# Values in two transfers, scales by one product with the identity, and a planner with other costs

## The chip, the cores and the metric

The kernel runs on one core of a Trainium2 chip. Its time is the device time of one execution in microseconds; the number compared is the median over runs. A profile of one further execution shows what each engine did: PE (TensorE, matmuls), PEld (its weight loads), ACT (ScalarE), DVE (VectorE), POOL (GpSimd) and SP (SyncE, which issues the DMAs here).

## The reference

Chunked attention with memory tokens, then a mixture of eight experts in which every token goes through every expert, weighted by a routing matrix that is normalised eight times by rows and columns.

```python
q, k, v: (4, 8, 768, 64)      mem_k, mem_v: (4, 8, 8, 64)
for c in range(24):                     # chunks of 32 rows
    k_ctx = k[:, :, max(0, 32*c - 16) : min(768, 32*c + 40)]   # v alike
    k_full = concat([mem_k, k_ctx])     # v alike
    a = softmax(q_c @ k_full.T / 8)
    out[:, :, chunk c] = a @ v_full
x = out.transpose(0, 2, 1, 3).reshape(3072, 512)

P = exp(x @ w_gate - max)               # (3072, 8)
for _ in range(8):
    P /= P.sum(1, keepdims=True) + 1e-9
    P /= P.sum(0, keepdims=True) + 1e-9
    P *= 3072 / 8
for e in range(8):                      # w1 (8, 512, 1024), w2 (8, 1024, 512)
    y += P[:, e:e+1] * (maximum(x @ w1[e], 0) @ w2[e])
```

## The kernel before

**Two kinds of work.** The attention goes over 24 blocks of 128 queries (six for each of the four batches, all eight heads together). A block has loads of q, k, a few extra rows of k (`load_extra`) and v; transposes of q and k on TensorE (tiles tq, tk, tx); small products of 32 rows for each chunk, head and block (`scores`, tile sp); maximum, difference and exponential; a transpose back (ta); the small products with the values (`values`, tile xp); division by the sum, and a transpose on VectorE into the tile xg, which holds 256 tokens. The experts go over 48 pairs of an expert and a unit of 512 tokens. All these products are made of numbers split into two float16 parts, high and low, so each product is three passes over matmuls of 256 columns (line 1676), and products of two by two blocks are made with seven block products in place of eight, with sums taken beforehand. The first unit (`first_unit`, tile pp for the hidden layer at line 2117) and the outputs of expert 0 (`plain_output`, tile yp at line 2200, 512 columns) are made without these sums, since the sums are not ready yet.

**Splitting.** `split` (line 540) makes the two parts of an operand: ScalarE writes the scaled high part (line 545), then VectorE the rest (line 553). `plain1` and `plain2` call it for expert 0's weights, in four parts fp = 0 to 3 of 512 KB each. `cut` (line 643) makes the sums of weights on GpSimd (line 651).

**Scales.** Every operand is scaled by a power of two that comes from the largest element, or from a bound on it. `scales` (line 462) turns a column of one bound per partition into one scale on all 128 partitions. In the kernel before: VectorE reduces to one column (473); TensorE transposes the column to a row (525, tile row); VectorE reduces the row (534) and rounds to a power of two (478, 479); TensorE spreads the number over 128 partitions by a product with ones (511, tile sp_x or sp_w); VectorE makes the inverse (484, 485). For the values, blocks 0 and 1 use a sum of absolute values on ScalarE (`total_v`, 1032), blocks 2 and 3 a maximum on VectorE (`most`, 1022).

**The values' tile.** It holds two windows in its 128 partitions: rows 0 to 63 for one chunk and rows 64 to 127 for the chunk two further on, each with eight memory rows ahead and 56 rows of v. `go_v` (line 987) loads them by four DMAs of 56 rows (8 heads x 256 bytes each). The memory rows are loaded once for a batch and slot by two small DMAs (`go_m`) and copied by GpSimd (`copy_m` 975, `take_m` 985); a later block of the same batch in the same slot finds them there.

**What sets the order.** The whole program is laid out beforehand by a planner (`Plan`, line 98). Every piece of work is a task with an engine, a cost in microseconds, those that it waits for, a priority (a due time) and its buffers. `Plan.run` walks a simulated clock, and for each engine takes the task that could start first, or the one with the lowest due time among those that can start now; each engine then has its instructions in that fixed order. The planner also models the DMA pipe (`dma=` cost of a transfer, `LANDS`, `READY`, `BEHIND`), the port that VectorE and GpSimd share (`port`, `held`), and the fetching of TensorE's own instructions (`count` and `earliest`: after 161 instructions and every 256 after that a fetch is asked for, which lands `FETCH` us later). Where it sees TensorE idle for over 0.4 us it puts in warming matmuls (`pad`, line 137; `fill`, line 452, tile warm), until the attention is over (`turn` sets `plan.fill` to None). The due times come from `START`, `TURN`, `UNIT`, `NEED` and the like (line 374).

Of the kernel before, what the change touches and what calls it, by code (L numbers as in the profile page):

```python
# [25 lines left out]
LANDS = 0.7  # L26
# [4 lines left out]
BLOCK = 256  # L31
ASKS = 161
HELD = 288
FETCH = 1.4
QUEUED = 6.0
FREE = 0.3


class Task:


    __slots__ = ("eng", "cost", "fn", "prio", "left", "ready", "end", "then", "takes", "frees", "n", "dma", "start", "size", "port")
# [55 lines left out]
class Plan:  # L98
# [16 lines left out]
    def add(self, eng, cost, fn, deps=(), prio=0.0, bufs=(), takes=None, frees=None, dma=0.0,  # L115
            size=0, port=None, since=0.0):
# [3 lines left out]
        t.size = size  # L120
# [16 lines left out]
    def pad(self, now, at):  # L137

        for banks in self.free.values():
            if banks and banks[0][0] <= now + 0.2:  # L140
                n = int((at - now - 0.1) * 0.8 / 0.11)
                if n > 0:
                    _, bank = heappop(banks)
                    self.fill(bank, n)
                    heappush(banks, (now + 0.11 * n + 0.2, bank))
                    self.count(2 * n, now, 0.11 * n)
# [12 lines left out]
    def earliest(self, t, at):  # L159


        for end, landed in self.fetches:
            if t.size and self.counted + t.size > end:
                at = max(at, landed - t.cost * (end - self.counted) / t.size)
        return at

    def run(self):
# [4 lines left out]
        for t in self.tasks:  # L172
            if t.left == 0:
                heappush(waiting[t.eng], (t.ready, t.n, t))
        left = len(self.tasks)
        while left:
            best = None
            for e in self.ENGINES:
# [26 lines left out]
                if pick is not None and (best is None or pick[0] < best[0]):  # L205
                    best = pick
            assert best is not None, "no task can start"
            at, t, heap = best
            if t.eng == "PE" and self.fill is not None and at - clock["PE"] > 0.4:
                self.pad(clock["PE"], at)  # L210
            heap[:] = [x for x in heap if x[2] is not t]
            heap.sort()
# [23 lines left out]
            else:  # L236
                clock[t.eng] = t.end = at + t.cost
            t.fn()
# [6 lines left out]
            lag = 0.0 if t.dma else 0.2 if t.eng == "PE" else 0.12  # L245
            for s in t.then:
                s.left -= 1
                late = lag
                if s.eng == t.eng and not t.dma:
                    late = 0.0  # L250
# [4 lines left out]
                if s.left == 0:  # L255
                    heappush(waiting[s.eng], (s.ready, s.n, s))
# [4 lines left out]
def tile_chunked_attn_sinkhorn_moe(  # L261
# [28 lines left out]
    P = 128  # L290
# [56 lines left out]
    idle = ident.bitcast(BF16)  # L347
    gate = amisc.tile([P, KT * E + CH - E], F32, name="gate")
# [25 lines left out]
    START, TURN, UNIT, AHEAD = 28.0, 62.0, 36.7, 48.0  # L374
# [77 lines left out]
    def fill(b, n):  # L452
        wp = banks(b).tile([P, 256], F32, tag=f"b{b}", name="warm")
        for _ in range(n):
            nc.tensor.matmul(wp, idle[:, 0:P], idle, start=True, stop=True)
# [6 lines left out]
    def scales(part, s, u, name, deps, prio, pool=None, shift=SHIFT):  # L462
# [26 lines left out]
        if pool is None:  # L489
# [14 lines left out]
        a = a[0:1]  # L504
        t = turned_max(m, a, t, pool, prio, name)
        t = add("DVE", 0.3, lambda: power(a), [t], soon, port=True)
        spread = bank(pool, [P, 1], f"sp_{name}")
        t = add(
            "PE",
            0.38,  # L510
            lambda: nc.tensor.matmul(spread.t, ones[0:1], a, start=True, stop=True),
            [t],
            prio - FIRM,
            takes=spread,
            size=4,
        )
        return add("DVE", 0.32, lambda: inverse(spread.t), [t], soon, frees=spread)

    def turned_max(m, a, t, pool, prio, name):
# [4 lines left out]
            0.35,  # L524
# [15 lines left out]
    def split(dst, src, s, deps, prio, costs, bufs=(), behind=()):  # L540
# [4 lines left out]
            lambda: nc.scalar.activation(dst(0), src(), AF.Copy, scale=s),  # L545
            deps,
            prio - 1.0,
            bufs,
        )
# [19 lines left out]
    def load(e, fp, which, prio, ahead="", since=0.0):  # L569
# [13 lines left out]
        cost = 1.7 if which == 1 else 1.5  # L583
# [18 lines left out]
    def total(fp, which, st, deps, prio):  # L602
# [11 lines left out]
        return add("ACT", 1.2, go, deps, prio, [st, first2[1]])  # L614
# [132 lines left out]
    def plain1(fp, st, ld, prio, behind=()):  # L747

        o = operands("w1", [P, 2, 7, 2, P], f"w1_0_{fp}")
        done = split(  # L750
# [5 lines left out]
            (1.15, 1.28),  # L756
            [st, o],
            behind,
        )
        wo[0, fp, 1] = (o, [done])  # L760
# [7 lines left out]
    def plain2(fp, st, ld, prio, before):  # L768

        done = split(  # L770
# [5 lines left out]
            (1.15, 1.28),  # L776
            [st, first2[fp]],
        )
        wo[0, fp, 2] = (first2[fp], [done])
# [15 lines left out]
    NEED = (4.0, 8.0, 29.0, 35.0)  # L795
# [32 lines left out]
    def load_extra(u):  # L828
# [10 lines left out]
        for n in range(n0, n0 + BU):  # L839
# [5 lines left out]
            def go(b=b, blk=blk, r0=r0, t0=t0):  # L845
# [7 lines left out]
                else:  # L853
# [10 lines left out]
                    dma=0.35,  # L864
# [7 lines left out]
        def part(r, loads, at, tx, takes):  # L872
            t = add("PE", 0.6, lambda: turn(r), loads, at, [kx, kxT], takes=takes, size=2 * HP)
# [1533 lines left out]
```

## Time and profile before

| | |
|---|---|
| median of three runs | 1905.94 us (1905.53 to 1907.52) |
| the profiled execution's own time | 1905.76 us |
| its span | 1904.0 us |
| granted TensorE clock, mean | 0.999 |
| busy ACT | 1028.3 us |
| DMA, mean over the span | 133 GB/s |

A profile page lists busy times; tables of stretches cut the span into windows; a list of waits says who waited for whom, with total, count and longest; a timeline lists instructions by start and length, merged where they repeat (xN); a bracket at its end tells how long the engine was idle before and what ended that. The chain is the work that ended last, followed back from the last instruction. "Issue" in it is time in which an engine waited for nothing that the profile shows. Durations of matmuls are modelled with their latency, so the rate of matmuls is read from their starts or their count in a stretch.

### The profile page before, as it was taken

Reading aid. Unit: us, or ns where it says so; the run is one execution under the profiler, and the core shown is the slowest. Engines: PE = TensorE matmul, PEld = TensorE weight load, DVE = VectorE, ACT = ScalarE, POOL = GpSimd, SP = SyncE. Lnnn points to the kernel's source line nnn. Section 1 sums busy time; section 2 is a strip of 40 time slices with the busy share of each in tenths; the row PEclk is TensorE's granted clock in tenths of the full one; section 3 lists DMA queues with packets and bytes.
Section 4 is the critical chain, followed back from the end, with each engine's and each line's share of the span. In section 5 each row is a group of like instructions: output and inputs, shape, how many; then the busy total and the mean of one; then the engine's idle time right before and its main releaser. Section 6 shows DMA issues by size and latency. Waiting matters only on the chain.

```text
span 1904.0 us, 46736 instructions
## 1 busy us (share of the span) xinstructions
PE 1889.6 (99%) x19471; PEld 1626.9 (85%) x19471; DVE 1455.4 (76%) x2417; ACT 1028.3 (54%) x2008; POOL 536.6 (28%) x576
## 2 busy tenths in 40 slices
PE   8999999999999999999999999999999999999999
PEld 6677676688888888888888888888888888888888
DVE  6886879778589866888679876897778885786575
ACT  6665455665466455556456545645555563554453
POOL 2430112544134211522224231342124231332112
PEclk9999999999999999999999999999999999999999
DMA  9967944543323541363235332255314633222322
GB/s 213 212 139 179 238 137 139 171 151 106 128 89 139 175 147 52 102 229 141 84 104 177 130 133 101 79 176 179 122 47 140 225 106 105 90 84 88 125 84 67
DMA packets 209101, 253.98 MB, mean 133 GB/s; under 512 B 108793, under 2 KB 142585, under 8 KB 204537
## 3 DMA queue, kind: packets, MB, share of 16 engines
q1 hardware_dynamic: 208888, 251.00, 42.3%
q8 instruction: 152, 2.49, 0.6%
q14 instruction: 61, 0.49, 0.1%
HBM read 187.51 MB, written 63.44 MB: 132 GB/s over the span
## 4 chain that ended last, share of the span: by engine, by line
PE 95%; DMA 2%; DVE 2%; issue 0%; ACT 0%; SPq 0%; POOL 0%; ACTq 0%; POOLq 0%; DVEq 0%
PE px L1676 25%; PE yx L1676 23%; PE pz L1676 13%; PE yz L1676 12%; PE py L1676 6%; PE yy L1676 6%; PE yp L2200 5%; PE pp L2117 1%; PE xp L1212 1%; PE sp L1134 1%; PE ta L1201 1%; DMA w1fm<-in_moe_w_dram 0%; PE tk L1075 0%; DMA w1f<-in_moe_w_dram 0%; PE tq L1071 0%; DVE x L553 0%
## 5 line engine op out<-in xcount | busy, mean ns | idle before, releaser
L1676 PEld LDWEIGHTS <-w 128*128 128x128 f16 x7896 | 771.3, 98 | 91.8 <-issue 1.0
L1676 PEld LDWEIGHTS <-h 128*128 128x128 f16 x7056 | 690.3, 98 | 80.0
L1676 PE MATMUL px<-x,w 128*128 128x256 f16 x4512 | 548.0, 273 | 0.1
L2003 POOL TENSOR_TENSOR acc<-acc,y 128x256 f32<-128x256 f32 x252 | 265.0, 1059 | 872.6 <-ACT y L1978 860.1
L1676 PE MATMUL yx<-w,h 128*128 128x256 f16 x4032 | 467.5, 273 | 0.0
L1725 ACT ACTIVATE q<-px 128x256 f32<-128x256 f32 x376 | 141.9, 380 | 288.1 <-PE px L1676 282.8
L1676 PE MATMUL pz<-x,w 128*128 128x256 f16 x2256 | 278.2, 273 | 0.1
L1676 PE MATMUL yz<-w,h 128*128 128x256 f16 x2016 | 233.8, 273 | 0.0
L1897 DVE TENSOR_TENSOR h<-ss,h 128x1024 f16<-128x1024 f32 x160 | 212.0, 1327 | 3.0 <-ACT h L1872 3.0
L1872 ACT CAST h<-ss 128x1024 f16<-128x1024 f32 x168 | 174.2, 1040 | 51.5 <-DVE ss L1835 51.5
L1847 ACT ACTIVATE h<-c 128x768 f16<-128x768 f32 x168 | 140.8, 838 | 108.5 <-DVE c L1735 108.3
L1880 DVE SCALAR_TENSOR_TENSOR h<-c,h 128x768 f16<-128x768 f32 x168 | 167.9, 1000 | 18.4 <-ACT h L1847 18.4
L1835 DVE SCALAR_TENSOR_TENSOR ss<-c,ss 128x256 f32<-128x256 f32 x336 | 171.5, 510 | 7.6
L1735 DVE SCALAR_TENSOR_TENSOR c<-px,q 128x256 f32<-128x256 f32 x188 | 77.8, 421 | 88.9 <-PE px L1676 84.7
L1676 PE MATMUL py<-x,w 128*128 128x256 f16 x1128 | 139.2, 273 | 0.0
L2200 PE MATMUL yp<-w,h 128*128 128x512 f16 x576 | 130.9, 379 | 0.0
L1835 DVE SCALAR_TENSOR_TENSOR ss<-c,h 128x512 f32<-128x512 f32 x168 | 126.1, 750 | 0.0
L1978 ACT ACTIVATE y<-yx,pscale 128x256 f32<-128x256 f32 x168 | 79.3, 472 | 83.7 <-PE yx L1676 78.7
L1676 PE MATMUL yy<-w,h 128*128 128x256 f16 x1008 | 116.9, 273 | 0.0
L1735 DVE SCALAR_TENSOR_TENSOR c<-py,q 128x256 f32<-128x256 f32 x188 | 77.7, 420 | 45.4 <-PE py L1676 42.5
L2200 PEld LDWEIGHTS <-h 128*128 128x128 f16 x576 | 55.5, 98 | 59.8
L545 ACT ACTIVATE w<-ws,sw 128x1024 f16<-128x1024 f32 (+1 forms) x64 | 69.5, 1090 | 67.1 <-POOL ws L651 66.4
(168 smaller groups left out, 1763.1 us busy)
## 6 DMA issues: line engine op xcount, KB each, us to landing
x<-xkeep SPq DMA_DIRECT2D x28, 1792.0 KB
akeep<-acc SPq DMA_DIRECT2D x168, 256.0 KB
acc<-akeep SPq DMA_DIRECT2D x168, 256.0 KB
w1f<-in_moe_w_dram SPq DMA_DIRECT2D x36, 512.0 KB
w2f<-in_moe_w_dram SPq DMA_DIRECT2D x32, 512.0 KB
w1fm<-in_moe_w_dram SPq DMA_DIRECT2D x28, 512.0 KB
w2fm<-in_moe_w_dram SPq DMA_DIRECT2D x28, 512.0 KB
xkeep<-x SPq DMA_DIRECT2D x6, 1792.0 KB
```

The lines of the kernel that those rows point to most:

```text
L545: lambda: nc.scalar.activation(dst(0), src(), AF.Copy, scale=s),
L1676: nc.tensor.matmul(dst.t, a, b, start=(not more and n == 0), stop=(n == end), skip_group_check=more,)
L1725: lambda: nc.scalar.activation(t.t, src.t, AF.Copy, scale=DOWN),
L1735: lambda: nc.vector.scalar_tensor_tensor(c.t[:, o], src.t, DOWN, q.t, op0=ALU.mult, op1=ALU.add),
L1835: lambda: nc.vector.scalar_tensor_tensor(dst(), src(), 0.0, other(), op0=ALU.max, op1=op),
L1847: lambda: nc.scalar.activation(h.t[:, 0, 0:3], c.t, AF.Relu),
L1872: lambda: nc.scalar.copy(h.t[:, 0, 3:7], ss.t),
L1880: lambda: nc.vector.scalar_tensor_tensor(h.t[:, 1, 0:3].rearrange("p a n -> p (a n)"), c.t.rearrange("p a n -> p (a n)"), 0.0, h.t[:, 0, 0 ...
L1897: lambda: spare.tensor_tensor(h.t[:, 1, 3:7], ss.t, h.t[:, 0, 3:7], op=ALU.subtract),
L1978: (lambda: nc.scalar.activation(t.t, src.t, AF.Copy, scale=f))
L2003: lambda: nc.gpsimd.tensor_tensor(acc.t[:, cols], acc.t[:, cols], q.t, op=ALU.add),
L2200: nc.tensor.matmul(py.t, hf.t[:, hl, where[fh], o : o + P], room(fp, WIDE * wl + DM * fh, WIDE * wl + DM * (fh + 1)), start=(fp == 0 and i ...
```

## The change

Six things at once, all in the making of the program:

1. `go_v` loads two DMAs per block, of up to 120 rows, which run on over rows 64 to 71; `go_m` loads the memory rows once; a new task `again_m` on GpSimd copies them over rows 64 to 71 behind the two DMAs, for every block. `values` and the bounds wait for it.
2. `scales` sends the column, broadcast to 128 columns, through one product with the identity, which gives the row on every partition; one task on VectorE makes the maximum, the power and the inverse there. The routing's own maximum keeps the old way.
3. Tasks can have a second engine (`also`): the high halves of expert 0's weights, two of the key copies and the first unit's relu may go to GpSimd where the planner finds it free sooner. For parts 2 and 3 of w1, `split_aside` puts all of it on GpSimd, but for the high half, which either of ScalarE and GpSimd may copy.
4. Blocks 2 and 3 of the values use `total_v` on ScalarE.
5. The warming matmuls have 512 columns in place of 256.
6. The planner's costs and due times: DMAs, products, the fetch of instructions, lags between engines; `START` 28 to 26, `TURN` 62 to 58, `AHEAD` 48 to 44; the gate's weights are due at 22 in place of 30; the routing is due 50 us behind the start of its unit in place of 30.

```diff
-LANDS = 0.7
+LANDS = 0.8
+GATE = 22.0
-FETCH = 1.4
+FETCH = 2.4
+REFILL = 1.4
+BACKLOG = 0.5
+OVERLAP = 0.07
+LAG = 0.04
+ROUTE = 50.0
+BESIDE = (2, 3), ()
...
-            queued = min(0.8 * max(self.pipe - when, 0.0), QUEUED)
+            queued = min(BACKLOG * max(self.pipe - when, 0.0), QUEUED)
...
-                at = max(at, landed - t.cost * (end - self.counted) / t.size)
+                done = t.cost * (end - self.counted) / t.size
+                if at + done < landed:
+                    at = landed + REFILL - done
...
                 clock[t.eng] = t.end = at + t.cost
+                if self.fill is not None and t.eng in ("ACT", "DVE"):
+                    clock[t.eng] -= OVERLAP
...
-        wp = banks(b).tile([P, 256], F32, tag=f"b{b}", name="warm")
+        wp = banks(b).tile([P, 2, 256], F32, tag=f"b{b}", name="warm")
...
-    START, TURN, UNIT, AHEAD = 28.0, 62.0, 36.7, 48.0
+    START, TURN, UNIT, AHEAD = 26.0, 58.0, 36.7, 44.0
...
+            lambda: nc.tensor.matmul(
+                row.t, m.broadcast_to([P, P]), ident, start=True, stop=True
+            ),
...
+        def here():
+            nc.vector.tensor_reduce(a, row.t, axis=AX.X, op=ALU.max)
+            power(a)
+            inverse(a)
+
+        return add("DVE", 0.85, here, [t], soon, port=True, frees=row)
...
+    def split_aside(dst, src, s, deps, prio, bufs=(), behind=()):
+
+        a = add(
+            "POOL",
+            1.1,
+            lambda: nc.gpsimd.tensor_scalar(src(), src(), s, None, op0=ALU.mult),
...
+        def high():
+            if b.eng == "POOL":
+                nc.gpsimd.tensor_copy(dst(0), src())
+            else:
+                nc.scalar.copy(dst(0), src())
+
+        b = add("ACT", 1.15, high, [a], prio - 1.0, bufs, also=("POOL", 1.1))
+        return add(
+            "POOL",
+            2.2,
+            lambda: nc.gpsimd.tensor_tensor(dst(1), src(), dst(0), op=ALU.subtract),
...
-    NEED = (4.0, 8.0, 29.0, 35.0)
+    NEED = (4.0, 8.0, 25.0, 31.0)
...
+        def again_m():
+            nc.gpsimd.tensor_copy(vt.t[KW : KW + NM, :, :, 0:D], vt.t[0:NM, :, :, 0:D])
...
-            for c in range(CB):
+            for c in range(CP):
                 r = NM + (LC if first and c == 0 else 0)
-                m = KW - r - (RC if last and c == CB - 1 else 0)
+                m = P - r - (RC if last and c == CP - 1 else 0)
...
-        lv = lm + [add("SP", CB, go_v, lv, at, [vt], dma=2.7)]
+        t = add("SP", CP, go_v, lv, at, [vt], dma=2.3)
+        lv = [*lm, add("POOL", 1.1, again_m, [*lm, t], at, [vt])]
...
-            vfound.append(add("DVE", 1.35, most_less, lv, at, [vt], since=START + 2.0))
+            vfound.append(add("ACT", 1.2, total_v, lv, at, [vt, first2[1]], since=START + 2.0))
...
-        hi = add(
-            "ACT",
-            0.63,
-            lambda: nc.scalar.activation(h.t[:, 0, where], c.t[:, 0:2], AF.Relu),
-            read,
-            now[0],
-            [h, c],
-        )
+        hi = add("ACT", 0.63, high, read, now[0], [h, c], also=("POOL", 0.75))
...
-        urgent = begin(LATE) + 30.0
+        urgent = begin(LATE) + ROUTE
...
         (),
-        30.0,
-        dma=0.3,
+        GATE,
+        dma=0.8,
```

More of the change, by code (lines that the diff above doesn't have):

```diff
@@ L31, with engines @@
 BLOCK = 256
+GATE = 22.0
 ASKS = 161
 HELD = 288
-FETCH = 1.4
+FETCH = 2.4
 QUEUED = 6.0
+REFILL = 1.4
+BACKLOG = 0.5
+OVERLAP = 0.07
+LAG = 0.04
 FREE = 0.3
+SUMS = 0.0
+ROUTE = 50.0
+BESIDE = (2, 3), ()
 class Task:
-    __slots__ = ("eng", "cost", "fn", "prio", "left", "ready", "end", "then", "takes", "frees", "n", "dma", "start", "size", "port")
+    __slots__ = ("eng", "cost", "fn", "prio", "left", "ready", "end", "then", "takes", "frees", "n", "dma", "start", "size", "port", "also")
+    def engines(self):
+        return (self.eng,) if self.also is None else (self.eng, self.also[0])
 class Past:
@@ L244, in run @@
                     heappush(self.free[b.group], (b.end, b.bank))
-            lag = 0.0 if t.dma else 0.2 if t.eng == "PE" else 0.12
+            near = LAG if self.fill is not None else 0.12
+            lag = 0.0 if t.dma else 0.2 if t.eng == "PE" else near
             for s in t.then:
@@ L347, in tile_chunked_attn_sinkhorn_moe @@
     idle = ident.bitcast(BF16)
+    twice = idle[:, None, :].broadcast_to([P, 2, 2 * P])
     gate = amisc.tile([P, KT * E + CH - E], F32, name="gate")
@@ L452, in fill @@
     def fill(b, n):
-        wp = banks(b).tile([P, 256], F32, tag=f"b{b}", name="warm")
+        wp = banks(b).tile([P, 2, 256], F32, tag=f"b{b}", name="warm")
         for _ in range(n):
-            nc.tensor.matmul(wp, idle[:, 0:P], idle, start=True, stop=True)
+            nc.tensor.matmul(wp, idle[:, 0:P], twice, start=True, stop=True)
     plan.fill = fill
@@ L503, in scales @@
             return add("DVE", 1.7, everywhere, [t], prio, port=True)
[L504 to L507, printed above, removed]
+        row = bank(pool, [P, P], f"row_{name}")
         t = add(
             "PE",
-            0.38,
-            lambda: nc.tensor.matmul(spread.t, ones[0:1], a, start=True, stop=True),
+            0.15,
+            lambda: nc.tensor.matmul(
+                row.t, m.broadcast_to([P, P]), ident, start=True, stop=True
+            ),
             [t],
             prio - FIRM,
-            takes=spread,
+            takes=row,
             size=4,
         )
-        return add("DVE", 0.32, lambda: inverse(spread.t), [t], soon, frees=spread)
+        def here():
[3 more added lines that the diff above has]
+        return add("DVE", 0.85, here, [t], soon, port=True, frees=row)
     def turned_max(m, a, t, pool, prio, name):
@@ L544, in split @@
             costs[0],
-            lambda: nc.scalar.activation(dst(0), src(), AF.Copy, scale=s),
+            high,
             deps,
@@ L612, in go @@
             )
-        return add("ACT", 1.2, go, deps, prio, [st, first2[1]])
+        return add("ACT", 1.2, go, deps, prio, [st, first2[1]], since=SUMS)
     def scale_w(e, which, deps, prio, pool=None, shift=SHIFT):
```

172 lines of the change are left out of this document (94 added, 78 removed).

## The prediction

> **What bounds the kernel now.** I read the page's first lines, then the stretches of the span, then TensorE's waits, then the chain of waits over the first 60 us.
>
> ```profile
> span 1904.0 us, 46736 instructions
> ...
> PE 1889.6 (99%) x19471; PEld 1626.9 (85%) x19471; DVE 1455.4 (76%) x2417; ACT 1028.3 (54%) x2008; POOL 536.6 (28%) x576
> ```
>
> ```profile
> 47.90:58.10 10.20, 8.26 (x205) 6.41 (x203) 9.37 (x18) 8.23 (x15) 0.72 (x1) 1.00 0.84 143
> ...
> 110.00:280.00 170.00, 169.34 (x3056) 123.91 (x3057) 128.12 (x240) 91.45 (x191) 19.29 (x25) 1.00 0.74 186
> ...
> 500.00:700.00 200.00, 200.00 (x1835) 179.24 (x1833) 160.21 (x255) 109.36 (x210) 64.42 (x69) 1.00 0.37 127
> ```
>
> The columns behind a window are its length, the busy time and count of PE, PEld, DVE, ACT and POOL, the granted clock, the DMA share and GB/s. From 110 us on TensorE is busy throughout: 169.34 of 170.00 us, later 200.00 of 200.00 with 1835 matmuls, 109 ns apiece. Those matmuls stay, so little can be won behind 110 us: the change acts on the first 110 us, and a microsecond in which TensorE does nothing useful there is a microsecond of the span, since no slack comes later. Part of the busy time is padding (the group of the warming matmuls), and TensorE's longest waits come beside it:
>
> ```profile
> L455 PE MATMUL warm<-ident 128*128 128x256 bf16 x119 | 16.9, 291 | 1.6 <-POOL ident masks.py:199 1.6
> ```
>
> ```profile
> PE pp L2117 <- ACT w L545: 2.1, 1, 2.1
> ...
> PE sp L1134 <- issue: 1.2, 1, 1.2
> PE xp L1212 <- issue: 1.0, 1, 1.0
> PE pp L2117 <- issue: 0.8, 2, 0.5
> ...
> PE lp L1472 <- DMA gate<-in_moe_w_gate_dram: 0.7, 1, 0.7
> ```
>
> So 16.9 us of warming matmuls and 5.8 us in these waits (2.1 + 1.2 + 1.0 + 0.8 + 0.7) are what the change can bite on, some 23 us; the attention of the first blocks must come ahead of the first expert matmul, so most of the padding stays. The chain (start, length, what) shows the way to that matmul:
>
> ```profile
> 16.37 4.98 DMA v_pair<-in_v_dram
> 21.64 0.96 issue
> ...
> 27.44 1.33 ACT x L545 x2
> 28.78 2.09 ACT w L545 x2
> 31.19 0.81 PE pp L2117 x6
> 32.68 5.35 PE pp L2117 x36
> ...
> 65.91 0.79 PE xp L1212 x53
> ```
>
> Block 1's values land at 21.35 us (16.37 + 4.98). TensorE's first expert matmul starts at 31.19, 9.84 us later.
>
> **A: the first expert matmul.** The change loads each block's values in two transfers of up to 120 rows in place of four of up to 56, and then GpSimd copies eight memory rows over rows 64 to 71 (again_m), which the attention's last product waits for. Rows for both, from the timelines of SyncE and GpSimd:
>
> ```profile
> 8.27 8.61 SPq L993 DMA_DIRECT2D v_pair<-in_v_dram x8
> ```
>
> ```profile
> 17.67 2.12 POOL L985 COPY x_room<-v_pair 8x1024 f32<-8x1024 f32 x2
> 50.26 0.72 POOL L1368 TENSOR_TENSOR xt<-xg 128x256 f32<-128x256 f32 x1 [30.47 <-DVE xg L1253]
> ```
>
> One copy of eight rows is 1.06 us (2.12 / 2); with a handover it puts about 1.2 us between landing and product. The eight issues took SyncE 8.61 us; four are fewer, but the rows per block grow from 224 to 240, 7% more packets, so I let the landing come 0.3 us earlier (bounds: 1.0 earlier, 0.5 later). The product can thus start near 22.2 us. The 0.96 us of "issue" in its middle should not return: padding matmuls are now twice as wide, so TensorE has fewer instructions by then.
>
> Behind it lie division, transpose and the scale of x, in the timeline of VectorE:
>
> ```profile
> 23.62 0.69 DVE L1233 TENSOR_TENSOR xq<-xp,rec 128x512 f32<-128x512 f32 x1
> ...
> 24.34 1.11 DVE L1253 STREAM_TRANSPOSE xg<-xq 128x512 f32<-128x512 f32 x1
> 25.36 0.24 DVE L534 TENSOR_REDUCE most_of<-row_x 1x1 f32<-1x128 f32 x1
> 25.63 0.14 DVE L478 TENSOR_SCALAR most_of<-most_of 1x1 f32<-1x1 f32 x1
> ...
> 25.88 1.26 DVE L553 SCALAR_TENSOR_TENSOR w<-w1f,sw,w 128x1024 f16<-128x1024 f32 x1
> ...
> 27.25 0.16 DVE L485 RECIPROCAL sx<-ux 128x1 f32<-128x1 f32 x1
> 28.20 1.42 DVE L553 SCALAR_TENSOR_TENSOR x<-xg,sx,x 128x512 f16<-128x512 f32 x2 [0.79 <-ACT x L545]
> ```
>
> From the reduction at 25.36 to the end of the reciprocal at 27.41 are 2.05 us, because the half-done scale goes back to TensorE (the spreading product) and VectorE does a weight of 1.26 us meanwhile. Now one product of the broadcast column with the identity gives the row of maxima on all 128 partitions, and reduction, two steps of the power and two of the inverse are one task: 0.24 + 2 x 0.14 + 2 x 0.16, about 0.85 us. So: product (0.79) 22.2 to 23.0, division to 24.1 (0.69 and two small steps), transpose to 25.2, scale to 26.1, ScalarE's first half (1.33 / 2) to 26.8, VectorE's (1.42 / 2) to 27.5, handover: first expert matmul at 27.7 against 31.19. Term A: -3.5 us, bounds -5.0 (the copy hidden as well) and -0.5 (only part of the detour saved). ScalarE's 2.09 us of weights ahead of that matmul no longer stand there: the plain weights of parts 2 and 3 go to GpSimd, idle for 30.47 us before 50.26.
>
> **B: the clock.** 36 expert matmuls took 5.35 us from 32.68; at 109 ns they take 3.9, so 1.4 us are lost. The stretches say why:
>
> ```profile
> 32.00:34.00 2.00, 2.00 (x13) 1.50 (x11) 2.00 (x3) 0.00 (x1) 0.00 (x0) 0.51 1.06 166
> 34.00:36.00 2.00, 2.00 (x13) 1.52 (x12) 1.80 (x3) 0.99 (x2) 0.00 (x0) 0.63 1.02 230
> ```
>
> The granted clock falls to 0.51 and 0.63 right after the wait of 2.1 us. If the plan sees that gap, it pads it, or the gap is gone: term B -1.4 us, bounds -1.4 and 0. The Trainium skill ("TensorE: Matmul & The Clock Gate", What's actually happening) has the clock halve only after an idle window of about 3.4 us; here 2.1 us of idling were followed by a halved clock, so the trace speaks for less. By that rule the dip would have no tie to this gap, B would be 0 and the gain 1.4 us smaller.
>
> **C: the first output product (58.07 us).** It waits for w2, whose scale takes the same detour:
>
> ```profile
> 49.88 0.27 PE L525 MATMUL row_w<-ident,most_of 128*1 128x128 f32 x1
> ...
> 58.07 2.75 PE L2200 MATMUL yp<-w,h 128*128 128x512 f16 x12
> ```
>
> ```profile
> 52.66 0.17 DVE L485 RECIPROCAL sw<-uw 128x1 f32<-128x1 f32 x1
> ```
>
> From 49.88 to 52.83 are 2.95 us; the new way takes the product's 0.27, a handover of some 0.2 and 0.85, about 1.3, so 1.6 less. Two maxima of values leave VectorE for ScalarE, whose high halves of w2, relu and small key copies may go to GpSimd; the gate's weights are asked for earlier. In 47.9 to 58.1 TensorE's busy time is 1.94 us short of 10.20, of which 0.7 is the gate, and some of the busy time is padding. Term C: -1.7 us, bounds -3.5 and 0.
>
> **D: TensorE's own instructions.** The page's DMA queues:
>
> ```profile
> q8 instruction: 152, 2.49, 0.6%
> ```
>
> 152 packets for 2 x 19471 matmuls and weight loads are one per 256 instructions. I take the waits called "issue" for late ones of these; 2.0 us (1.2 + 0.8) are not in A. The planner's new costs for that fetch (2.4 us in place of 1.4, and 1.4 more where it ran dry) let it place a score block elsewhere; but a shifted plan can run dry at new places. Term D: -0.5 us, bounds -2.0 and +1.5.
>
> **E: what is added.** again_m runs for all 24 blocks, where blocks that kept their memory rows had nothing: 24 x 1.06 = 25 us of GpSimd, which is 28% busy. Queued behind it on GpSimd are the weights' sums (L651); on TensorE, whose order is fixed, everything after that block's product stands behind it. From block 6 on values land long before use, so it costs nothing there unless GpSimd lags; in the ramp it can. Term E beyond what A holds: +1.0 us, bounds 0 and +4.
>
> Routing later and the other planned costs behind 280 us lie beside a full TensorE: 0. If that cover failed, the first scaled accumulators would wait.
>
> Sum: -3.5 - 1.4 - 1.7 - 0.5 + 1.0 = -6.1 us. The profiled execution took 1905.76 us (span 1904.0 and 1.76 around it), 0.18 under the median of 1905.94: 1905.76 - 6.1 = 1899.66, and with the 0.18 that the median lies above it 1899.8 us.
>
> **Rivals.**
>
> *The gain is given back.* In the first 60 us the DMA engines are nearly full:
>
> ```profile
> 50.00:60.00 10.00, 8.07 (x139) 5.68 (x138) 9.17 (x18) 9.31 (x16) 1.13 (x2) 1.00 0.95 160
> ```
>
> If the loads of blocks 2 to 7, and not the scales, set the middle of the ramp, TensorE starts earlier and waits longer at 47 to 58 us. For it: a share of 0.95 here, and the wait on the gate's load. Against: VectorE and ScalarE are at 9.2 and 9.3 of 10 there. A and C then cancel against new waits, B and D's -0.5 stay: -1.9, 1903.9 us.
>
> *GpSimd is in the way (slower).* Plain w1 of parts 2 and 3 now is a product in place, a copy and a difference over 1024 columns. The nearest row, 0.72 us for 256 columns, makes 2.9 each, 17.3 us for six; the diff's own costs (1.1, 1.1, 2.2) make 8.8. The scale of w1 is there at 20.7 us (its reciprocal below), and part 3 is wanted 7.9 us (72 matmuls of 109 ns) behind the start at 27.7, at 35.6. So it decides at 14.9 us for the six: above, TensorE waits, up to 2.4 us and 1.1 for an again_m among them. Meanwhile GpSimd makes VectorE wait:
>
> ```profile
> 20.51 0.16 DVE L485 RECIPROCAL sw<-uw 128x1 f32<-128x1 f32 x1
> ...
> 75.48 0.95 DVE L553 SCALAR_TENSOR_TENSOR w<-ws,sw,w 128x256 f16<-128x256 f32 x1
> ...
> 86.81 0.47 DVE L553 SCALAR_TENSOR_TENSOR w<-ws,sw,w 128x256 f16<-128x256 f32 x1
> ```
>
> ```profile
> 74.97 1.18 POOL L651 TENSOR_TENSOR ws<-w1f 128x256 f32<-128x256 f32 x1
> ```
>
> The same VectorE instruction took 0.95 us beside GpSimd and 0.47 alone. One GpSimd step of 2.9 us ahead of x's half leaves A at -0.6; part 3 late, +3.5; B and C not won; later copies late, +2. Sum +4.9: 1910.7 us. The Trainium skill ("SBUF — State Buffer", Who interferes with whom) calls the port that the two share a lock held for the whole instruction; the rows of 0.95 and 0.47 agree.
>
> *The plan shifts as a whole.* If the padding shrinks too, by some 3 us because the new plan has real work in those gaps: -9.1, 1896.7 us. For it, 16.9 us of padding; against, little but attention can fill it.
>
> **How the numbers follow.** Forecast 0.55, given back 0.23, GpSimd in the way 0.13, whole shift 0.09. About 0.2% (3.8 us) is what a measurement of this kernel can tell from no change: faster is below 1902.1, slower above 1909.8. Of the forecast's 0.55, 0.45 goes to faster and 0.10 to the same, as the upper bounds of E and D and the lower gain of A reach past 1902.1; of the given-back case 0.05 to faster, 0.16 to the same, 0.02 to slower; of the slower rival 0.02 to the same, 0.11 to slower; the whole shift to faster. Together 0.59, 0.28, 0.13. The range, 1894.5 to 1908.0, takes in the whole shift, the given-back case and most of the unknown costs' bounds (all at their ends would be 1893.8 and 1910.8), and leaves out the slower rival.
>
> **What the changed profile would show.** Right: the first expert matmul (pp) at 26.5 to 28.5 us; granted clock 1.00 in 32 to 36; no spreading products of the scales; the first output product (yp) at 53 to 55.5; less padding and "issue" before 110. Wrong: pp still near 31 with GpSimd busy throughout 20 to 36, waits of the attention's last product on GpSimd, DMA waits at 45 to 58 that grew, or a gap in TensorE behind 110 us.

## The result and the profile after

The kernel after took 1915.37 us, the median of four runs (1914.02 to 1918.82), beside 1906.73 us for the kernel before on the same chip: a ratio of 1.005 with a 95% interval of 1.0036 to 1.0064. One of the four runs of before took 3984.7 us and is left out of the ratio; the median of the other three is 1905.94. After is slower by about half a per cent, some 9 us; the forecast was 6 us faster, in a range that ended at 1908.0. The profiled execution took 1914.02 us, with a span of 1912.2.

The first lines of the page after and its stretches (columns as in the prediction):

```profile
span 1912.2 us, 46548 instructions
...
PE 1891.0 (99%) x19398; PEld 1621.3 (85%) x19398; DVE 1458.9 (76%) x2411; ACT 1020.9 (53%) x1992; POOL 585.4 (31%) x612
```

```profile
34.00:36.00 2.00, 0.40 (x2) 0.14 (x2) 1.06 (x2) 2.00 (x6) 1.30 (x2) 0.69 0.93 201
36.00:38.00 2.00, 2.00 (x10) 1.66 (x10) 1.77 (x2) 1.12 (x3) 0.59 (x1) 0.50 1.21 291
47.90:58.10 10.20, 10.20 (x264) 8.92 (x254) 9.33 (x21) 9.49 (x21) 7.96 (x6) 1.00 1.07 180
110.00:280.00 170.00, 165.00 (x2977) 120.95 (x2975) 128.92 (x235) 92.49 (x187) 32.93 (x43) 1.00 0.71 181
```

TensorE has 73 matmuls fewer than before (the padding got wider), so it is not more work that takes the time. The row of 110 to 280 us is the one to compare: 165.00 us busy, where before had 169.34. That stretch was full, and now has holes of 5 us. TensorE's waits from 110 us on, after and then before, say what they wait for:

```profile
PE sp L1190 <- issue: 2.5, 2, 2.1
PE px L1732 <- DVE c L1791: 1.5, 3, 1.1
PE yp L2256 <- issue: 1.2, 1, 1.2
PE px L1732 <- ACT q L1781: 1.0, 2, 0.6
PE pz L1732 <- DVE c L1791: 0.7, 1, 0.7
PE xp L1268 <- issue: 0.6, 1, 0.6
PE pz L1732 <- ACT q L1781: 0.3, 1, 0.3
```

```profile
PE xp L1212 <- DVE s L1154: 0.7, 1, 0.7
```

7.8 us of waits in place of 0.7; 4.3 of them are "issue", time in which TensorE waits for nothing that the profile shows.

To place all of the loss, I summed from the starts of TensorE's instructions in each trace how much longer each stretch of one tile took than the same stretch usually does (gaps), and added the time in warming matmuls. Up to 110 us this is 31.5 us before and 30.9 after; from 110 to 420 us it is 5.5 before and 15.0 after. The ramp is as long as it was, and all of the loss, some 9 us, lies where the prediction had nothing. The tables below give these two sums for most kernels, as "ramp" and "later". They are of the one profiled execution, which for some kernels lies 3 to 4 us off the median (copies in after's order 1919.10, planner alone 1908.64).

The first expert matmul came late because GpSimd was in the way. The chain of waits (start, length, what) towards the first expert matmul of after:

```profile
20.42 1.16 POOL w L600
21.58 1.74 issue
23.34 1.04 POOL v_pair L1046
24.38 0.08 issue
24.47 6.53 POOL w1f L574 x2
31.02 0.03 ACT w L584
31.04 0.93 issue
31.97 1.15 ACT w L669 x2
33.14 1.15 ACT w L669 x2
34.29 0.62 ACT x L602
34.91 0.03 issue
34.94 0.99 DVE x L616
```

The groups of GpSimd's new work (busy, mean ns of one, idle before):

```profile
L2207 POOL TENSOR_SCALAR h<-c 128x512 f16<-128x512 f32 x4 | 6.9, 1732 | 9.3 <-ACT c L2196 9.3
...
L574 POOL TENSOR_SCALAR w1f<-w1f,sw 128x1024 f32<-128x1024 f32 x2 | 6.5, 3266 | 0.1
...
L600 POOL TENSOR_SCALAR w<-w2f,sw 128x1024 f16<-128x1024 f32 x2 | 5.7, 2844 | 0.3 <-DMA q<-in_q_dram 0.3
...
L582 POOL CAST w<-w1f 128x1024 f16<-128x1024 f32 x1 | 1.0, 1029 | 0.0
```

The planner has 0.75, 1.1 and 1.2 us for the first three (a relu, a product in place, a product into float16). Of these only the cast (1.1) takes what it was planned at. What that did to TensorE, in the timelines of ScalarE, VectorE and TensorE:

```profile
31.02 1.05 ACT L584 CAST w<-w1f 128x1024 f16<-128x1024 f32 x1 [3.05 <-POOL w1f L574]
```

```profile
28.86 0.16 DVE L509 RECIPROCAL sx<-ux 128x1 f32<-128x1 f32 x1
...
52.94 0.16 DVE L509 RECIPROCAL sw<-uw 128x1 f32<-128x1 f32 x1
```

```profile
24.43 1.13 PE L1268 MATMUL xp<-v_pair,at 64*32 64x65 f32 x62 [0.75 <-POOL v_pair L1046]
...
34.95 0.37 PE L2173 MATMUL pp<-x,w 128*128 128x256 f16 x1 [3.03 <-ACT x L602]
...
51.36 0.39 PE L532 MATMUL row_w<-ident,most_of 128*128 128x128 f32 x2
...
59.18 1.03 PE L2256 MATMUL yp<-w,h 128*128 128x512 f16 x4
```

The scale of x is there at 29.02 us. Its use on ScalarE stands in a fixed queue behind a cast that waits 3.05 us for GpSimd, and behind two bounds of w2, and starts at 34.20. The first expert matmul comes at 34.95 us, 3.8 later than before.

### The profile page after: what moved, and what is told of

It reads as the page before. It is cut to its first block, busy times and chain, and to the rows that moved or that the text cites. A ratio compares the mean times of both kernels' runs of the same rounds, so it can differ in the third digit from the quotient of the medians.

```text
span 1912.2 us, 46548 instructions
## 1 busy us (share of the span) xinstructions
PE 1891.0 (99%) x19398; PEld 1621.3 (85%) x19398; DVE 1458.9 (76%) x2411; ACT 1020.9 (53%) x1992; POOL 585.4 (31%) x612
## 4 chain that ended last, share of the span: by engine, by line
PE 92%; DVE 4%; DMA 1%; POOL 1%; issue 1%; ACT 1%; POOLq 0%; DVEq 0%; ACTq 0%
PE px L1732 25%; PE yx L1732 23%; PE pz L1732 12%; PE yz L1732 11%; PE py L1732 6%; PE yy L1732 6%; PE yp L2256 5%; DVE w L616 1%; PE xp L1268 1%; PE sp L1190 1%; POOL ws L714 1%; DMA w1fm<-in_moe_w_dram 1%; DVE x L616 1%; PE ta L1257 0%; PE tq L1119 0%
## 5 line engine op out<-in xcount | busy, mean ns | idle before, releaser
L2059 POOL TENSOR_TENSOR acc<-acc,y 128x256 f32<-128x256 f32 x252 | 271.2, 1084 | 872.5 <-ACT y L2034 859.1
L1891 DVE SCALAR_TENSOR_TENSOR ss<-c,ss 128x256 f32<-128x256 f32 x336 | 175.6, 523 | 7.2
L1891 DVE SCALAR_TENSOR_TENSOR ss<-c,h 128x512 f32<-128x512 f32 x168 | 121.1, 721 | 0.0
L2256 PEld LDWEIGHTS <-h 128*128 128x128 f16 x576 | 55.5, 98 | 63.4 <-DVE h L2216 2.3
```

The costliest lines, as they stand in the source:

```text
L1891: lambda: nc.vector.scalar_tensor_tensor(dst(), src(), 0.0, other(), op0=ALU.max, op1=op),
L2059: lambda: nc.gpsimd.tensor_tensor(acc.t[:, cols], acc.t[:, cols], q.t, op=ALU.add),
L2256: nc.tensor.matmul(py.t, hf.t[:, hl, where[fh], o : o + P], room(fp, WIDE * wl + DM * fh, WIDE * wl + DM * (fh + 1)), start=(fp == 0 and i ...
```

## The experiments

Each kernel ran beside the kernel before on its chip; the ratio is to that. Kernels that differ in any planned cost or task have another order of instructions throughout; where an order was kept, the text says so.

### Does GpSimd's slowness make the loss?

Four kernels. The first keeps the order of after and has plain copies where GpSimd multiplies or takes a relu; the second lets the planner know GpSimd's true costs; the third gives the planner the DMA costs of before; the fourth is the kernel before with one planned cost changed by a hundredth.

```diff
# copies in after's order
-    lambda: nc.gpsimd.tensor_scalar(src(), src(), s, None, op0=ALU.mult),
+    lambda: nc.gpsimd.tensor_copy(dst(0), src()),
-    nc.gpsimd.tensor_scalar(dst(0), src(), s, None, op0=ALU.mult)
+    nc.gpsimd.tensor_copy(dst(0), src())
-    nc.gpsimd.tensor_scalar_max(h.t[:, 0, where], c.t[:, 0:2], 0.0)
+    nc.gpsimd.tensor_copy(h.t[:, 0, where], c.t[:, 0:2])
# true costs: 1.1 -> 3.3 (L574), 1.2 -> 2.9 (L600), 0.75 -> 1.6 (relu)
# DMA costs of before: LANDS 0.7, BACKLOG 0.8, xkeep 7.0, gkeep 2.1, akeep 1.3
# sham of before: a block of scores at 0.89 in place of 0.9
```

Copies in after's order:


> Every engine keeps the changed kernel's order; only GpSimd's products with a scale (two of parts 2 and 3 of w1, one high half of w1, two of w2) and its two relus become plain copies to float16 of the same shape, so these leave out the scaling and the relu of expert 0. Theory 1 (these products take 2.9 to 3.3 us where the plan has 1.1 to 1.2, and ScalarE's queue stands still behind one): the first expert matmul comes at 30 to 31.5 us in place of 34.95, TensorE's waits behind 110 us stay at about 8 us, and the kernel gains 3 to 4.5 us on the changed one: 1911 to 1912. Theory 2 (the loss is all in the stretch behind 110 us, and an earlier start is only padded or waited away there): within 1 us of the changed kernel, 1914.5 to 1916. Theory 3 (the shared port is the cause of the waits behind 110): no change there, as these products lie ahead of it.

GpSimd's true costs:


> The changed kernel with the planner told what the profile shows for GpSimd's products: 3.3 us for the product in place, 2.9 for a high half, 1.6 for the relu. Theory 1: the plan no longer stops ScalarE behind them; the first expert matmul at 28 to 31 us, and 3 to 6 us gained: 1909 to 1912. Theory 2: the plan is only another draw; within 2 us of the changed kernel, on either side.

DMA costs of before:


> The changed kernel with the planner's view of the DMA queue as it was before (landing 0.7, stores and loads of x 7.0 in place of 4.8, accumulators 1.3 in place of 0.95, halves of x 2.1 in place of 1.5, and 0.8 in place of 0.5 of the backlog added to a fetch of TensorE's instructions). Theory 1 in its second half (behind 110 us TensorE waits for instruction fetches that stand behind stores, and for ScalarE and VectorE that stand behind late loads, since the plan expects both too early): TensorE's waits behind 110 us fall from about 8 us to 1 to 3, while the first expert matmul stays near 35; 1908 to 1911. Theory 2' (the lags between engines, or GpSimd's new copies, cause them): the waits stay at 6 to 9 us, 1913 to 1917.

Sham of before:


> The kernel before with one planned cost of the score products at 0.89 us in place of 0.9, as the change has it, and nothing else: a plan of the same quality, differently drawn. If any new plan costs as much as the change did, it is 3 to 9 us slower than the kernel before; if the change's loss has causes of its own, it stays within 2.5 us on either side: 1903.5 to 1909.

| beside before at 1906.96 us | median us | ratio (95%) | ramp | later |
|---|---|---|---|---|
| copies in after's order | 1915.47 | 1.0046 (1.0032 to 1.0061) | 32.5 | 15.6 |
| GpSimd's true costs | 1924.51 | 1.0091 (1.0076 to 1.0106) | 32.9 | 16.4 |
| DMA costs of before | 1921.34 | 1.0079 (1.0063 to 1.0096) | 31.1 | 14.5 |
| sham of before | 1908.48 | 1.0010 (1.0001 to 1.0020) | 32.0 | 7.5 |

Cheap copies bring nothing by themselves: the first expert matmul starts at 30.24 us, and TensorE then waits elsewhere. TensorE's timeline in this kernel shows one place:

```profile
86.75 0.34 PE L1268 MATMUL xp<-v_pair,at 64*32 64x65 f32 x16
90.25 0.98 PE L1268 MATMUL xp<-v_pair,at 64*32 64x65 f32 x48 [3.15 <-issue]
```

It stops in the middle of a tile, after 16 of 64 small products, for 3.15 us of "issue". True costs in the planner make it worse, not better (with 7 us more of gaps behind 420 us). Both kernels planned anew from after missed every range that was forecast for them; the sham of before stayed within its 2.5 us. So the explanation "GpSimd alone" fell.

### Which part of the change?

The values' and the scales' part put on the kernel before, and the planner's costs alone; then the latter with two groups of constants set back.

```diff
# values and scales: go_v, go_m, again_m, bounds on ScalarE, turned_max; planned costs as before
# planner alone: all new costs and lags, wide padding; old values, scales, due times
# old lags, on planner alone
-                    clock[t.eng] -= OVERLAP
-            near = LAG if self.fill is not None else 0.12
+            near = 0.12
...
# old fetch model, on planner alone
-FETCH, REFILL, BACKLOG = 2.4, 1.4, 0.5
+FETCH, REFILL, BACKLOG = 1.4, 0.0, 0.8
```

Values and scales:


> The kernel before with the values in two transfers, again_m, all four values' bounds on ScalarE, and the scales by one product; the planner, its costs of everything else and the due times as before. Theory P (the planner's new costs and lags are the loss): 1903 to 1909, no waits on VectorE's or ScalarE's reads in the expert products behind 110 us. Theory S (the new pieces of work are the loss: the copy behind each block, GpSimd on the shared port): 1911 to 1917 with such waits.

Planner alone:


> The kernel before with the planner's new costs, lags, fetch model and the wider padding matmuls; its due times, values, scales and engines as before. Theory P: 1911 to 1918, with 2 to 5 us of waits on VectorE and ScalarE in the expert products behind 110 us. Theory S: 1903 to 1909.

Planner with old lags:


> As f2_planner, with the lags between engines and between instructions of one engine as before (0.12 and 0, no overlap taken off). If the short lags (0.04, and 0.07 taken off each step of ScalarE and VectorE) make the plan expect results too early, the waits of f2_planner behind 110 us go and it gains 3 us or more on f2_planner; if the fetch model or the DMA costs do it, it stays within 2 us of f2_planner.

Planner with the old fetch model:


> As f2_planner, with the fetch of TensorE's instructions planned as before (1.4 us, 0.8 of the backlog, nothing more where it ran dry). If the new fetch model makes the plan expect TensorE later than it is, so that ScalarE and VectorE put other work ahead of its reads, it gains 3 us or more on f2_planner and the waits behind 110 us go; else within 2 us of it.

Then each of the two parts by itself, the scales on top of the planner's costs, and a sham of after: its own planned cost of a block of scores back from 0.89 to 0.90.

Scales on before:


> The kernel before with one part of the change alone: a scale's maxima are turned by one product with the identity (hunk of turned_max); all planned costs, the values and the copies stay. Theory S (the new pieces of work themselves are the loss): the scales lose nothing, they are shorter by 1.2 us at three places, so 1904 to 1907 beside 1907. Theory R (any edit redraws the whole plan, and a redraw of this plan lies on average above it, by some 0 to 12 us, wherever the edit was): 1908 to 1917, with new waits at places that no scale touches.

Values on before:


> The kernel before with the values' part alone: two transfers, again_m, and all four bounds of the values on ScalarE; scales, planned costs and copies stay. Theory S: this is where the 9.8 us of both parts together came from, so 1914 to 1918, with waits on again_m or on ScalarE's bounds. Theory R: anywhere from 1907 to 1917, and together with the scales alone not adding up to 9.8.

Planner and scales:


> The kernel with the planner's new costs (1904.8) plus the scales by one product. Theory S: shorter by up to 1 or 2 us, 1902.5 to 1905. Theory R: a redraw again, 1904 to 1917, not the same difference as the scales made on the kernel before.

Sham of after:


> The kernel after with one planned cost changed back by a hundredth (a block of scores at 0.90 us in place of 0.89): no new work, another draw of the plan. Theory S: 1914 to 1917, as after. Theory R: off by over 2.5 us to either side of 1915.4, between 1904 and 1920.

| | median us | before beside it | ratio (95%) | ramp | later |
|---|---|---|---|---|---|
| values and scales | 1916.84 | 1907.04 | 1.0056 (1.0040 to 1.0072) | 34.2 | 12.2 |
| planner alone | 1904.80 | 1907.04 | 0.9992 (0.9982 to 1.0001) | 30.5 | 8.9 |
| planner, old lags | 1918.73 | 1907.04 | 1.0067 (1.0052 to 1.0082) | 33.1 | 16.1 |
| planner, old fetch | 1912.36 | 1907.04 | 1.0029 (1.0016 to 1.0042) | 28.7 | 12.7 |
| scales on before | 1913.88 | 1907.41 | 1.0031 (1.0020 to 1.0041) | 35.4 | 11.4 |
| values on before | 1915.02 | 1907.41 | 1.0038 (1.0023 to 1.0053) | 32.5 | 11.4 |
| planner and scales | 1908.49 | 1907.41 | 1.0005 (0.9996 to 1.0014) | 28.2 | 10.2 |
| sham of after | 1921.02 | 1907.41 | 1.0069 (1.0054 to 1.0084) | 33.4 | 22.6 |

In the first four, theory S (the new pieces of work are the loss) had forecast the two halves: 1916.84 and 1904.80 lie in its ranges. The two that set constants back lost 13.9 and 7.6 us on the planner alone, where a gain of 3 or no change was forecast. In the last four S fell for the scales: alone they add 6.5 us although they remove work, and on the planner's costs 3.7. The values alone add 7.6, in the ranges of both theories; both together 9.8, not 14. A hundredth in one cost adds 5.6 to after (4.2 by the distances from before). So a loss needs no added work: the scales add none. Whether the values' work adds to the loss is neither shown nor excluded, since no run put them alone on the planner's costs. What held is that any edit redraws the order, and that the time varies by where things then fall, mostly behind 110 us. TensorE's timeline of the sham of after shows again a stop in the middle of a tile, after 63 of 64 products:

```profile
114.45 0.84 PE L1190 MATMUL sp<-kC,qT 64*32 64x64 f32 x63
118.83 0.21 PE L1190 MATMUL sp<-kC,qT 64*32 64x64 f32 x1 [3.54 <-issue]
```

### What are the stops?

After has such a stop as well, in the timelines of TensorE and SyncE:

```profile
155.85 0.41 PE L1190 MATMUL sp<-kC,qT 64*32 64x64 f32 x21
158.35 0.68 PE L1190 MATMUL sp<-kC,qT 64*32 64x64 f32 x43 [2.09 <-issue]
```

```profile
148.91 0.34 SPq L1381 DMA_DIRECT2D xkeep<-x  x1
149.48 0.32 SPq L2281 DMA_DIRECT2D akeep<-acc  x1
```

and in the DMA view the stretch 137.5 to 156 us has one queue only, while 156 to 158 us has a fetch of instructions on queue q8:

```profile
q1 hardware_dynamic: 4267, 3.32, 61.9%
```

```profile
q1 hardware_dynamic: 1741, 0.44, 116.5%
q8 instruction: 1, 0.02, 3.0%
```

Counted in the traces, a fetch that finds the queue free starts within a few instructions of TensorE's 161st, or of every 256th behind that, and stops like this one come exactly 288 instructions later, at the end of a block: TensorE carries on for 288 instructions behind the point at which a fetch is asked for. Here that point is at 150.3 us, just behind the issue of a store of 128 rows of 14336 bytes (xkeep, a scaled unit kept for the later experts) and of one of 256 KB (akeep). The fetch starts at 156.05, when the packets of both are through (154.64 and 156.05), and lands at 157.02; TensorE has issued its last instruction at 156.05 too and goes on at 158.35, 1.3 us behind the landing. The Trainium skill ("Runtime: NRT & Kernel Launch", Instruction fetch mechanics) has instructions refilled in blocks of 256 through a DMA queue, at a cost mostly hidden: the blocks agree with the prediction's 152 packets, and that the cost is hidden does not hold here.

Three such stops behind a store of xkeep stand in after (2.30, 1.45 and 0.84 us by the starts), 7.9 us of them in the copies kernel, 7.1 in the sham of after, 1.4 in before.

The test keeps four kernels' orders to the instruction and cuts only that store to a quarter:

```diff
-nc.sync.dma_start(xkeep[u], x.t.rearrange("p a o k n -> p (a o k n)"))
+nc.sync.dma_start(xkeep[u][:, :1792], x.t.rearrange("p a o k n -> p (a o k n)")[:, :1792])
...
-x.t.rearrange("p a o k n -> p (a o k n)"), xkeep[nxt]
+x.t.rearrange("p a o k n -> p (a o k n)").rearrange("p (r m) -> p r m", r=4),
+xkeep[nxt][:, None, :1792].broadcast_to([P, 4, 1792])
```

After with the cut store:


> The kernel after, instruction for instruction in its own order, with each store of a scaled unit (xkeep) cut from 14336 to 3584 bytes a partition; it leaves out three quarters of that scratch, and the later load reads the first quarter four times. The trace of after has three stalls of TensorE for its instructions behind such stores, 2.30 + 1.45 + 0.84 = 4.6 us. Theory Q (the new order puts instruction fetches behind these stores, and that is over half of the 8.4 us lost): these three stalls go and the time falls to about 1911. Theory W (the stalls are only where a wait shows that would come anyway, on copies, values or keys): the stalls go and other waits take their place, 1914 to 1916.

Copies in after's order, with the cut store:


> The kernel of plain copies in after's order (1915.5), with the same cut of the stores (leaves out scaling and relu on GpSimd, and three quarters of the scaled units' scratch). Its trace has stalls of 3.37 + 2.30 + 1.45 + 0.76 = 7.9 us behind such stores. Theory Q: these were what gave back the earlier start, so 1907 to 1909. Theory W: 1913 to 1916.

Before with the cut store:


> The kernel before with the same cut of the stores, the control (leaves out three quarters of the scaled units' scratch). Its trace has one stall behind such a store, 1.40 us at 88 us. Theory Q: 1905 to 1906 beside 1907. Theory W: 1907. If it falls by as much as after does, the stores cost both kernels alike and explain no difference.

Sham of after with the cut store:


> The sham of after (1921.0; one planned cost 0.01 us higher) with the same cut of the stores (leaves out three quarters of the scaled units' scratch). Its trace has 3.75 + 2.60 + 0.78 = 7.1 us of stalls behind such stores, 2.5 more than after. Theory Q: 1913 to 1915, so that most of its 5.6 us over after go. Theory W: 1919 to 1921.

| beside before at 1907.78 us | median us | against its own order uncut | ratio to before (95%) | ramp | later |
|---|---|---|---|---|---|
| after, cut | 1910.11 | -5.3 | 1.0013 (1.0003 to 1.0022) | 31.1 | 10.9 |
| copies, cut | 1906.29 | -9.2 | 0.9994 (0.9985 to 1.0004) | 28.5 | 9.2 |
| before, cut | 1906.54 | -1.2 | 0.9991 (0.9982 to 1.0000) | 31.5 | 6.3 |
| sham of after, cut | 1910.16 | -10.9 | 1.0011 (1.0002 to 1.0021) | 30.6 | 8.6 |

The third column compares medians from different chips; by the distances from before it is -7.1, -10.0, -1.2 and -11.2. All four fell as theory Q says, and the sham's extra 5.6 us are gone. Not all lie in Q's ranges: the copies kernel and the sham fell further than it forecast, and before with the cut store lies between Q's 1906 and W's 1907. All stops of over 0.3 us at ends of blocks behind 110 us, added up, went from 5.2 to 1.6 us in after, from 5.4 to 0.3 in the copies kernel and from 7.7 to none in the sham; before had none there, and one of 0.6 with the cut store. The tile that stopped in after now runs through in TensorE's timeline, and the stretch 110 to 280 us is at 167.79 us busy (165.00 uncut); the copies kernel is at 168.60:

```profile
156.00 0.86 PE L1190 MATMUL sp<-kC,qT 64*32 64x64 f32 x64
```

```profile
110.00:280.00 170.00, 167.79 (x2992) 122.42 (x2990) 134.75 (x239) 92.92 (x188) 37.31 (x47) 1.00 0.63 150
```

```profile
110.00:280.00 170.00, 168.60 (x2929) 121.74 (x2928) 135.60 (x244) 94.78 (x192) 37.12 (x45) 1.00 0.63 149
```

Three of the falls (5.3, 9.2 and 10.9) are larger than the stops alone (4.6, 7.9 and 7.1), so the shorter store spares more than the stops; it also frees the queue for other transfers, which no run took apart.

The last two ask whether the packets' size or the bytes in the queue hold the fetch. They keep all work and bytes, and the order; a gap behind every 3584 bytes of the scratch turns 128 packets of 14336 into 512 of 3584.

```diff
-dram.tile([P, 2 * 7 * 2 * GT], F16, name=f"xkeep_{u}")
+dram.tile([P, 4, 7 * GT + 32], F16, name=f"xkeep_{u}")
```

After, small packets:


> The kernel after in its own order with all its work: the scratch of the scaled units gets a gap behind every 3584 bytes, so that each store and load of a unit goes in 512 packets of 3584 bytes in place of 128 of 14336; the bytes stay. Theory P (a fetch waits for the size of the packets ahead of it on its queue's engine): the three stalls of 4.6 us behind stores shrink to about a quarter, 1911 to 1912.5. Theory B (it waits for the bytes queued ahead, whatever their packets): they stay, 1914 to 1917.

Planner alone, small packets:


> The kernel before with the planner's new costs alone (1904.8 us, the fastest that computes everything), with the same packets of 3584 bytes. Its trace has stalls of 2.50 and 0.82 us behind such stores and other transfers. Theory P: up to 2.5 us less, 1902 to 1904, faster than before and after. Theory B: 1904 to 1906.

After with small packets took 1914.93 us (ratio 1.0043, 1.0029 to 1.0057), the planner's kernel 1906.29 (0.9996, 0.9988 to 1.0005), beside 1907.37 for before. TensorE's waits in the former still show the stop, now the largest of all:

```profile
PE sp L1190 <- issue: 3.7, 1, 3.7
```

The first lies in theory B's range, the second just above both ranges. In the planner's kernel the stop of 2.50 us came at 0.56, but its fetch too started only behind the store's last packet (157.66 behind 157.19; with large packets 160.42 behind 158.37). So what is queued ahead counts, not its packets, as far as these sizes and one profiled execution of each show. This repairs nothing. No kernel that computes everything beat both; the planner's costs alone (1904.80) cannot be told from the kernel before.

## Why the prediction was wrong

**The sum that holds.** Cutting the stores takes 5.3 us off after and 1.2 off before, so they explain 4.0 of the loss. With the stores cut, copies in place of GpSimd's products take another 3.8 (1910.11 to 1906.29). What is left stands 0.25 under before with the cut store (1906.54). 4.0 + 3.8 - 0.25 is 7.6 us, the distance of 1915.37 from 1907.78. By the three runs of before beside it, after stands 9.4 us above, and the stores' share is then 5.9; each term has some 2 to 3 us of uncertainty, by the intervals. The split hangs on the order of the two steps: with whole stores, copies took nothing off (1915.47), so the 3.8 show only where the stores no longer hold up the fetches.

**What bounds the kernel: the step that failed.** "Those matmuls stay, so little can be won behind 110 us", and then "Routing later and the other planned costs behind 280 us lie beside a full TensorE: 0." Little can be won in a full stretch; much can be lost. The order before had its stops at ends of blocks in the first 110 us (five over 0.3 us, 6.2 us together), and none behind; a redrawn order puts a fetch behind a store in any place. Ramp -0.6 in place of -6.1, later +9.5 in place of 0.

**A (-3.5, bounds -5.0 and -0.5): wrong in sign, +3.8.** Block 1's values landed at 21.5 us (21.05 forecast), and the one-product scale is shorter, though by less than worked out: w2's took 1.74 us from its product at 51.36 to its reciprocal's end (2.95 before; 1.3 forecast). But the spare copy stood behind a product on GpSimd (its timeline follows) and ended at 24.4, not 22.2, and the scale of x came at 29.0, not 26.1:

```profile
20.42 2.86 POOL L600 TENSOR_SCALAR w<-w1f,sw 128x1024 f16<-128x1024 f32 x1 [1.93 <-DVE sw L509]
23.34 1.03 POOL L1046 COPY v_pair<-v_pair 8x1024 f32<-8x1024 f32 x1
```

The other 4.3 us of the miss are ScalarE's. What failed is "ScalarE's 2.09 us of weights ahead of that matmul no longer stand there": in their place stood a cast that waited for GpSimd. With cheap copies the matmul came at 30.24, only 0.95 earlier than before, near A's smaller end: TensorE waited for loads of q and k there (0.60 and 0.59 us).

Those 2.09 us were not a wait for weights in the first place. Counted as above, TensorE stopped in before at an end of a block, from 28.82 to 31.19 us; the fetch, asked for at 20.84, ran from 28.35 to 29.79, and TensorE went on 1.4 us behind its landing. In the sham of before the same matmul starts at 30.76, while ScalarE is still at the second of these weights, until 30.98 (timelines of ScalarE and TensorE):

```profile
28.81 2.17 ACT L545 ACTIVATE w<-w1f,sw 128x1024 f16<-128x1024 f32 x2
```

```profile
30.76 0.81 PE L2117 MATMUL pp<-x,w 128*128 128x256 f16 x6 [1.68 <-ACT w L545]
```

So the profile put a late fetch down to ScalarE, and so did the prediction. With that fetch where it stood, an earlier scale of x alone could not have started the matmul before 31.

**B (-1.4): not won.** The granted clock is 0.69 and 0.50 in 34 to 38 us, and 0.50 and 0.60 in 38 to 42, behind a wait of 3.03 us that the plan did not see and so did not pad. It had fallen once before, behind waits of 1.02 and 0.75 us, so that after lost more to the clock than before did:

```profile
24.00:26.00 2.00, 1.57 (x65) 1.40 (x66) 2.00 (x2) 1.59 (x3) 1.91 (x2) 0.63 0.94 314
26.00:28.00 2.00, 2.00 (x10) 1.37 (x9) 1.51 (x6) 1.37 (x5) 2.00 (x1) 0.52 1.13 337
```

The Trainium skill ("TensorE: Matmul & The Clock Gate", What's actually happening) puts the window at about 3.4 us idle; the wait of 3.03 us, like the 2.1 us of before, was shorter and the clock fell.

**C (-1.7): won, then returned.** The first output product came at 59.18, not 53 to 55.5, but the idle time ahead of it is gone: 10.20 of 10.20 us busy in 47.9 to 58.1, with no padding. It came back right behind, where VectorE is full and TensorE waits 1.77 us for the low part of the relu's output:

```profile
74.61 1.68 PE L2256 MATMUL yp<-w,h 128*128 128x512 f16 x7 [1.77 <-DVE h L2216]
```

**D (-0.5, bounds -2.0 and +1.5): the mechanism named, its place and size not.** "A shifted plan can run dry at new places" is what happened, but the bound came from the ramp. The 2.0 us of "issue" that it took for late fetches were too few: with the wait that was put down to ScalarE they were 6.2 in the ramp of before, and after has none over 0.3 us there. Waits called issue behind 110 us were 0 before and 4.3 after, and the runs that redrew the order moved the sum of later gaps from 5.5 up to 22.6.

**E (+1.0): about right.** TensorE waited 0.75 us for again_m; the copy's own delay behind GpSimd's product is in A.

**The rivals.** "GpSimd is in the way" had the right sign, the right price of a product (2.9 us by 256 columns; 2.86 and 3.27 measured) and the sign named for it, pp late with GpSimd busy. Its six steps took 12.9 us and not 17.3 (products 6.53, casts 1.03 and 1.05, the latter on ScalarE, differences 2.12 each), less than the 14.9 at which it was to decide; what decided was one product that ScalarE's fixed queue waited for. By itself it is worth nothing in the time, with the stores cut 3.8. It got 0.13 because the diff's own cost of 1.1 was given weight beside a row of the trace that said 2.9. "The gain is given back" is what the copies kernel with cut stores shows: 28.5 us in the ramp, 3.0 fewer than before, and 1906.29 in all. The shift of the whole plan was taken as a gain only; as a loss it was no rival at all.

**What stays open.** Of the later gaps with cut stores (10.9 after, 6.3 before), waits of the expert products for `c` on VectorE are the largest; no run took these apart. In the kernels with the scales, the values or both put on before, at most 0.7 us of the later gaps are stops at ends of blocks, so the 6.5 to 9.8 us that they lose have other causes. That redrawn orders lie above before more often than below (11 of the 12 kernels that were planned anew and compute everything, two of them by under 0.2%) is an observation; nothing here shows why before's order has no such stops behind 110 us.

## What to carry to other kernels

Where a planner lays out the whole program, a full engine is not a stretch in which nothing can happen: each edit redraws what comes later, so try a sham edit first and know its scatter (here 1.5 and 4 to 6 us) before crediting a part. Take a cost for an engine from the nearest row of the trace, not from the number planned. And where TensorE stops inside a tile with nothing to wait for, look for its instruction fetch on the DMA queues and for the store that was issued just before; do the same where a wait is put down to an engine that another run shows still at work when the wait ends.

## What the hardware showed that was not expected

- GpSimd's product of 128x1024 float32 with a column of scales took 2.84 us into float16 and 3.27 in place; a cast of the same size took 1.03.
- A fetch of TensorE's instructions started 5.7 us behind its asking when stores of 1792 and 256 KB were issued 1.4 and 0.8 us ahead of the asking, and splitting the store's packets fourfold did not help.
- Once out of instructions, TensorE went on 1.3 to 1.4 us behind the fetch's landing (three stops in after, the three longest in before).
